# Chunk 0's second layer by Strassen's identity, and a later load of five sequences' beacon keys

## The chip, the cores and the metric

The kernel runs on one core of one Trainium2 chip. The metric is the device time of one execution in microseconds (us). A core has five engines with a queue of instructions each: PE (TensorE, matmuls; its weight loads are listed apart as PEld), DVE (VectorE), ACT (ScalarE), POOL (GpSimd) and SP (SyncE, which only issues transfers here). Engines wait for each other by semaphores; within a queue the order of the program is kept.

## The reference

Attention over 8 sequences of 8 heads, 576 positions and width 64, with 16 beacon keys and values per head that every position may see, and then two dense layers over all 4608 positions:

```python
k_all = np.concatenate([beacon_k, k], axis=2)
v_all = np.concatenate([beacon_v, v], axis=2)
scores = scale * np.matmul(q, k_all.transpose(0, 1, 3, 2))
causal[:, Nb:] = np.triu(np.ones((S, S), dtype=bool), k=1)
scores = np.where(causal, -1000000000.0, scores)
a = softmax(scores)                                      # over the keys
x = np.matmul(a, v_all).transpose(0, 2, 1, 3).reshape(B * S, H * D)   # 4608 x 512
h = x @ w_in                                             # 512 x 2048
g = np.maximum(0.01 * h, h)
return (g @ w_out).astype(np.float32)                    # 4608 x 512
```

## The kernel before

**Attention.** Heads go in 32 pairs, four to a sequence: pairs 0 to 3 are sequence 0, pairs 12 to 15 sequence 3. A pair's queries and keys are turned so that the width lies on the partitions: for pairs 0 to 7 by PE (`t_q`), from pair 8 on by SP's transposing transfers (`turn_pair`, L179) out of `q_nat` and `k_nat`, which POOL's casting transfers load (`load_natural`, L171). The 16 beacon keys take the first 16 columns of a pair's key tile. They come from `bkT`, which holds all sequences' beacon keys turned: `load_beacon_k` (L185) loads them, `cast_beacon_k` (L188) makes them bf16, `beacon_transposes` turns them, two PE transposes a sequence (L194) and two DVE copies out of PSUM (L203), and `beacon_columns` (L229, on POOL) copies a pair's 16 columns. Sequences 0 and 1 are loaded at the start, 2 to 7 in one load behind the first half of `w_out`.

From pair 8 on, scores are made in tiles of 512 columns that run on from one pair into the next; a `block` is three tiles (PE L314, exp on ACT L329 and L333), followed by the causal masks on POOL (`triangle`, L289). `value` multiplies with the values (PE L359), and DVE normalises (L388, L389). The result is turned into `xT` by PE for pairs up to 7 (L405, copy L410), by SP's transfers after that (L417, L425).

**Dense layers.** The 4608 positions go in nine chunks of 512. The first layer (`moe1`, L442) makes one block of 128 of the 2048 inner columns in a step, four 128x512 matmuls, and ACT's Prelu writes it to `gT` (L450). The second layer of chunks 1 to 8 follows Strassen's identity in Winograd's form on 2 x 2 blocks: seven products instead of eight. `PRODUCTS` is their order; a product is two steps (one for each 128 tokens) of eight 128x256 matmuls (L544). Its operands are blocks of `gT` and `w_out_sb` or sums of them: `weight_sums` makes t1, t2, t4 (`w_sum`) and overwrites b12 in `w_out_sb` with b22 - b12; `token_sums` makes s1, s2, s4 (`gsum`) and overwrites a21 in `gT` with a11 - a21, in two slices, one for each half of the first-layer blocks. `combine` puts the products together (ACT copies L575, DVE additions L572) and stores four quarters of the chunk. Chunk 0's second layer is plain: `moe2_plain` makes 128 tokens in four steps of four 128x512 matmuls (L519), DVE copies the bank (L528), and SP stores it (L529). `weight_sums(0)` stands at `t0`, behind pair 7's turning, and `weight_sums(1)` behind chunk 0's last step.

**Order.** The order on all engines is written out by hand up to pair 7 (strings that `run` reads: `u` is a first-layer step, `d` a second-layer step, `s` scores, `m` masks, `v` values, `x` turning a pair's result, `T` turning a pair's inputs, `b` beacon columns, `N` loads, `t` weight sums). From pair 8 on it is a list of events sorted by a due place, measured in pairs; between two events first- and second-layer steps (`up`, `down`) are filled in so that the steps that are open are spread evenly. `up` and `down` each issue one waiting DVE sum (`add_due`) ahead of their matmuls. `late` holds additions that are put off to the next step. PSUM has four single banks (`ps_one`) for everything but the scores' double banks.

Of the kernel before, what the change touches and what calls it, by code (L numbers as in the profile page):

```python
# [15 lines left out]
def kernel(  # L16
# [11 lines left out]
    nc = tc.nc  # L28
# [433 lines left out]
    def weight_sums(part):  # L462
        b11, b12 = w_out_sb[:, 0:HF, 0:HD], w_out_sb[:, 0:HF, HD:DM]
        b21, b22 = w_out_sb[:, HF:NF, 0:HD], w_out_sb[:, HF:NF, HD:DM]
        t1, t2, t4 = (w_sum[:, i] for i in range(3))
        tt = nc.vector.tensor_tensor
        if part == 0:
            tt(out=t1, in0=b12, in1=b11, op=SUB)
            tt(out=t2, in0=b22, in1=t1, op=SUB)
            tt(out=t4, in0=b21, in1=t2, op=SUB)  # L470
        else:
            tt(out=b12, in0=b22, in1=b12, op=SUB)
# [3 lines left out]
    def token_sums(i, lo, hi):  # L476
        if i not in sums:
            sums[i] = [sum_tile(n).rearrange("p (c t) -> p c t", c=HF) for n in range(3)]
        g, s = gT[i], sums[i]
        a11, a12 = g[:, lo:hi, 0:HT], g[:, HF + lo : HF + hi, 0:HT]  # L480
        a21, a22 = g[:, lo:hi, HT : 2 * HT], g[:, HF + lo : HF + hi, HT : 2 * HT]
        s1, s2, s4 = (s[n][:, lo:hi] for n in range(3))
        return [
            dict(out=s1, in0=a21, in1=a22, op=ADD),
            dict(out=s2, in0=s1, in1=a11, op=SUB),
            dict(out=a21, in0=a11, in1=a21, op=SUB),
            dict(out=s4, in0=a12, in1=s2, op=SUB),
        ]

# [18 lines left out]
    PRODUCTS = (1, 4, 6, 2, 7, 5, 3)  # L508
    banks, parts = {}, {}

    def ND(i):
        return NF if i == 0 else 2 * len(PRODUCTS)

    def moe2_plain(i, t, quarter):
        if quarter == 0:
            banks["a"] = ps_one.tile([128, 512], FP32, name="acc", tag="one")
        acc = banks["a"]
        for fc in range(quarter * 4, quarter * 4 + 4):
            nc.tensor.matmul(  # L519
                out=acc,  # L520
                lhsT=gT[i][:, fc, t * 128 : (t + 1) * 128],
                rhs=w_out_sb[:, fc],
                start=(fc == 0),
                stop=(fc == NF - 1),
            )
        if quarter == 3:
            osb = opool.tile([128, DM], FP32, name=("p1", "p4", "p5", "u3")[t], bufs=1)
            nc.vector.tensor_copy(out=osb, in_=acc)  # L528
            nc.sync.dma_start(out=out[i * 512 + t * 128 : i * 512 + (t + 1) * 128], in_=osb)  # L529

    def moe2(i, n2):
        if i == 0:
            moe2_plain(i, n2 // 4, n2 % 4)
            if n2 == NF - 1:
                weight_sums(1)
            return
        n, tile = PRODUCTS[n2 // 2], n2 % 2
# [16 lines left out]
        elif tile == 1:  # L554
            combine(i, n, acc, (0, 2))
# [3 lines left out]
    def add_late(now=False):  # L559
        while late and (now or late[0][0] < done1[0] + done2[0]):  # L560
            late.pop(0)[1]()

# [231 lines left out]
    def up():  # L794
# [11 lines left out]
        if i1 and n % (2 * SLICE) == 2 * SLICE - 1:  # L806
# [107 lines left out]
    with order:  # L914
# [18 lines left out]
        load_beacon_k(2, B, nc.gpsimd)  # L933
        run("s5.0 s5.1 m5.0 u u u s5.2 s5.3 q6 k6 m5.1 m5.2 o1 u u s6.0 s6.1 m6.0 u v4.0 u v4.1 y4 N8.0 N8.1 u s6.2 s6.3 q7 k7 m6.1 m6.2 u")
        cast_beacon_k(2, B, nc.gpsimd.tensor_copy)
        run("u v5.0 u v5.1 N9.0 s7.0 s7.1 m7.0 d x5 v6.0 v6.1 T8 d s7.2 s7.3")
        beacon_transposes(2, B)
        run("m7.1 m7.2 N9.1 u b8.2 b9.2 b10.2 b11.2 x6 v7.0 T9 v7.1 d d d N10.0 N10.1 d V2.0 V2.1 x7 t0 T10")
# [27 lines left out]
        for g in range(FIRST, NG):  # L966
# [5 lines left out]
            if g > FIRST + 3:  # L972
                events.append((g - 2.5, 0, run, ("b%d.2" % g,)))
# [15 lines left out]
        for b in range(2, B):  # L989
            for n in range(2 if b == 2 else 0, NKB):  # L990
                events.append((4 * b + ((-0.1, 0.1)[n > 3] if b == 2 else 0.3 * n - 0.4), 6, load_v_cast, (b, n)))
        events.sort(key=lambda e: e[:2])
# [49 lines left out]
```

## Time and profile before

| what | value |
|---|---|
| median of 3 executions | 325.34 us (325.18 to 329.55) |
| the profiled execution | 325.64 us, of which the span of the instructions is 323.8 us |
| granted TensorE clock | 1.0 |
| chunk 0's second layer | 47.3 to 73.5 us |
| scores of block 3 (with pair 11's first columns) | 77.1 to 78.5 us |
| POOL, 58 to 64 and 76 to 88 us | busy the whole time |
| DVE, 53.7 to 78.5 us | busy 11.3 of 24.8 us |
| first product of chunk 1 | from 88.4 us |

The span is cut into 40 slices, with each engine's busy share in tenths:

```
PE   7999999999999999999999999999999999999995
DVE  3464245508255244444443454525464689577954
ACT  4968962387855786478746874687458547455510
POOL 8895868999996787659875977666221000000000
```

In the lists of groups and in the timelines a row has the start, the length, the engine, the line, the operation with its tiles and shapes, the count, and in brackets the idle time ahead of it with what ended it. Matmuls are pipelined: a row's length holds the tail of its last matmul, so lengths are read from one start to the next. In the chain of work that ended last, a row has start, length and what the time was spent on.

### The profile page before, as it was taken

The page shows a single profiled execution, that of the slowest core. Times are in us where ns is not written, and L with a number is a line of the kernel's source. Part 1 is how long each engine was busy: PE and PEld are TensorE (multiplying, and loading weights), DVE is VectorE, ACT ScalarE, POOL GpSimd, SP SyncE. Part 2 cuts the span into 40 slices and gives each one's busy share as a digit, 9 for nine tenths or more (in the row PEclk, how much of TensorE's full clock was granted, in tenths as well). Part 3 has the DMA queues.
Part 4 walks back from the last instruction along what each step waited for, and adds up shares of the span by engine and source line. Part 5 has one row for each costly group of instructions (what it writes and reads, how often), then busy time and mean ns, then how long its engine had stood idle before and what let it go on. Part 6 is the DMA issues. An engine that isn't in the chain of part 4 may idle for free.

```text
span 323.8 us, 8701 instructions
## 1 busy us (share of the span) xinstructions
PE 314.3 (97%) x3468; PEld 219.1 (68%) x3494; DVE 168.0 (52%) x341; ACT 203.8 (63%) x346; POOL 184.3 (57%) x354
## 2 busy tenths in 40 slices
PE   7999999999999999999999999999999999999995
PEld 4575555444588557855788888656875697688784
DVE  3464245508255244444443454525464689577954
ACT  4968962387855786478746874687458547455510
POOL 8895868999996787659875977666221000000000
PEclk9999999999999999999999999999999999999999
DMA  8999999999999999999999999999222100200123
GB/s 137 129 189 192 124 214 140 169 177 188 135 152 160 216 138 129 114 186 97 141 176 174 99 143 119 188 128 129 44 81 82 26 2 32 75 25 2 65 67 130
DMA packets 155256, 39.78 MB, mean 123 GB/s; under 512 B 142368, under 2 KB 152480, under 8 KB 155216
## 3 DMA queue, kind: packets, MB, share of 16 engines
q0 software_dynamic: 99824, 18.54, 91.1%
q1 hardware_dynamic: 55120, 20.62, 38.3%
q8 instruction: 27, 0.44, 0.6%
q14 instruction: 13, 0.11, 0.1%
q10 hardware_dynamic: 272, 0.07, 0.1%
HBM read 37.22 MB, written 9.44 MB: 144 GB/s over the span
## 4 chain that ended last, share of the span: by engine, by line
PE 72%; DMA 14%; POOL 9%; ACT 3%; issue 1%; DVE 0%; POOLq 0%; ACTq 0%; SPq 0%
PE acc L442 24%; PE acc L544 19%; PE sc L544 11%; PE av L359 6%; PE sc L314 5%; PE acc L663 5%; DMA w_out_sb<-in_moe_w_out_dram 4%; DMA gsum<-in_k_dram 4%; POOL aT L289 3%; DMA k_nat<-in_k_dram 3%; DMA v_aug<-in_v_dram 2%; ACT aT L333 2%; DMA kT<-k_nat 2%; POOL gsum L158 1%; POOL v_aug L214 1%
## 5 line engine op out<-in xcount | busy, mean ns | idle before, releaser
L442 PE MATMUL acc<-xT,w_in_sb 128*128 128x512 bf16 (+1 forms) x537 | 116.5, 354 | 1.5 <-ACT aT L329 0.3
L450 ACT ACTIVATE gT<-acc 128x512 bf16<-128x512 f32 x124 | 70.8, 623 | 33.1 <-PE acc L442 32.6
L289 POOL TENSOR_SCALAR_AFFINE_SELECT aT<-aT 128x256 bf16<-128x256 bf16 (+2 forms) x160 | 59.7, 403 | 51.4 <-ACT aT L329 31.5
L442 PEld LDWEIGHTS <-w_in_sb 128*128 128x128 bf16 x560 | 51.7, 98 | 43.9 <-issue 2.9
L544 PEld LDWEIGHTS <-gT 128*128 128x128 bf16 x512 | 48.7, 98 | 7.7 <-issue 1.8
L333 ACT ACTIVATE aT<-sc 128x1024 bf16<-128x1024 f32 (+3 forms) x64 | 51.7, 892 | 0.0
L329 ACT ACTIVATE aT<-sc 128x512 bf16<-128x512 f32 (+3 forms) x64 | 29.0, 520 | 27.8 <-PE sc L314 27.8
L388 DVE RECIPROCAL rec<-av 128x6 f32<-128x6 f32 (+1 forms) x64 | 12.0, 187 | 65.0 <-PE av L359 64.4
L359 PEld LDWEIGHTS <-aT 128*128 128x128 bf16 (+1 forms) x960 | 36.9, 98 | 9.2 <-issue 1.4
L544 PEld LDWEIGHTS <-gsum 128*128 128x128 bf16 x384 | 36.5, 98 | 6.5 <-issue 0.4
L359 PE MATMUL av<-v_aug,aT 128*128 128x65 bf16 (+1 forms) x960 | 39.8, 194 | 0.8 <-DMA v_aug<-in_v_dram 0.4
L214 POOL DMA_DIRECT2D v_aug<-in_v_dram x40 | 34.1, 856 | 4.2 <-DMA w_in_sb<-in_moe_w_in_dram 3.8
L171 POOL DMA_DIRECT2D k_nat<-in_k_dram x48 | 34.8, 730 | 0.9 <-DMA w_out_sb<-in_moe_w_out_dram 0.3
L171 POOL DMA_DIRECT2D q_nat<-in_q_dram x48 | 34.8, 729 | 0.6 <-issue 0.4
L389 DVE TENSOR_TENSOR x_nat<-av,rec 128x384 bf16<-128x384 f32 (+1 forms) x64 | 31.4, 491 | 2.2
L544 PE MATMUL acc<-w_out_sb,gT 128*128 128x256 bf16 x240 | 28.9, 273 | 0.4 <-ACT gT L450 0.4
L276 ACT ACTIVATE aT<-sc 128x1024 bf16<-128x1024 f32 (+3 forms) x32 | 26.0, 874 | 4.7 <-PE sc L267 2.5
L314 PE MATMUL sc<-qT,kT 64*128 64x80 bf16 (+22 forms) x384 | 22.2, 250 | 0.3
L314 PEld LDWEIGHTS <-kT 64*128 64x128 bf16 x384 | 12.8, 94 | 11.2 <-issue 7.6
L544 PE MATMUL acc<-w_sum,gsum 128*128 128x256 bf16 x160 | 20.1, 273 | 0.0
L575 ACT COPY p<-acc 128x512 f32<-128x512 f32 x15 | 9.1, 604 | 16.8 <-PE acc L544 16.8
L785 DVE TENSOR_TENSOR gsum<-gT 128x1024 bf16<-128x1024 bf16 x16 | 11.0, 688 | 15.7 <-ACT gT L450 15.7
(95 smaller groups left out, 339.0 us busy)
## 6 DMA issues: line engine op xcount, KB each, us to landing
out_dram<-p SPq DMA_DIRECT2D x26, 256.0 KB, 3.2
q_nat<-in_q_dram POOLq DMA_DIRECT2D x48, 72.0 KB, 5.5
k_nat<-in_k_dram POOLq DMA_DIRECT2D x48, 72.0 KB, 5.3
v_aug<-in_v_dram POOLq DMA_DIRECT2D x24, 128.0 KB, 6.5
w_in_sb<-in_moe_w_in_dram POOLq DMA_DIRECT2D x2, 1024.0 KB, 12.4
w_out_sb<-in_moe_w_out_dram POOLq DMA_DIRECT2D x2, 1024.0 KB, 12.1
out_dram<-u SPq DMA_DIRECT2D x8, 256.0 KB, 2.7
gsum<-in_q_dram POOLq DMA_DIRECT2D x8, 144.0 KB, 7.1
```

The lines of the kernel that those rows point to most:

```text
L171: nc.gpsimd.dma_start(out=t[:, :, par], in_=(q, k)[which][b, 2 * hp + par].rearrange("(t p) d -> p t d", p=NR),)
L214: nc.gpsimd.dma_start(out=dst[lo : ROWS[c], c, :, 0:D], in_=v[b, :, OFF[c] : OFF[c] + n].rearrange("h p d -> p h d"),)
L276: nc.scalar.activation(out=aT[:, :, c0 : c0 + w], in_=sc[:, :, 0:w], func=AF.Exp, scale=0.125)
L289: nc.gpsimd.affine_select(out=view, in_=view, compare_op=ALU.is_ge, fill=0.0, base=128 - n if lo == 0 else 0, channel_multiplier=-1, patte ...
L314: nc.tensor.matmul(out=(sc[par] if apart else sc[:, par])[:, at : at + b - a], lhsT=kT[ps_, c * 128 : (c + 1) * 128], rhs=qT[ps_, q0 : q0 ...
L329: nc.scalar.activation(out=probs[g][:, par, lo:hi], in_=sc[par][:, at : at + hi - lo], func=AF.Exp, scale=0.125)
L333: nc.scalar.activation(out=probs[g][:, :, lo:hi], in_=sc[:, :, at : at + hi - lo], func=AF.Exp, scale=0.125)
L359: nc.tensor.matmul(out=avv[:, n, 0 : D + 1], lhsT=aT[0 : ROWS[c], par, a0 : a0 + 128], rhs=va[0 : ROWS[c], c, 2 * hp + par, :], start=(c = ...
L389: nc.vector.tensor_tensor(out=x_nat[:, t0:t1].rearrange("p t e d -> p (t e) d"), in0=avv[:, :, 0:D], in1=rec[:, n0:n1, None].to_broadcast( ...
L442: nc.tensor.matmul(out=acc[:, lo:hi], lhsT=w_in_cols(fc, j), rhs=xT[:, j, x0 : x0 + hi - lo], start=(j == 0), stop=(j == NJ - 1), skip_gro ...
L450: nc.scalar.activation(out=gT[i][:, fc, :], in_=acc, func=AF.Prelu, alpha=0.01)
L544: nc.tensor.matmul(out=acc[:, lo : lo + HD], lhsT=left(i, n, fc, tile), rhs=right(n, fc), start=(lo == 0 and fc == 0), stop=(fc == HF - 1) ...
```

## The change

Chunk 0's second layer takes the seven products too, in an order of its own (`FIRST_PRODUCTS`) and with a combination of its own (`combine_first`). Its token sums are made as soon as half of the first-layer blocks are there and again after the rest, with s4 ahead of a11 - a21. The four weight sums are spread over chunk 0's steps: t1 ahead of pair 8's turning, t2 behind pair 7's turning, b22 - b12 behind product 6's addition, t4 behind product 7's. Chunk 0 has 14 second-layer steps instead of 16, and as the steps are spread by their number, nine instead of eight of chunk 1's first-layer steps stand ahead of block 3's scores. The load of sequence 2's beacon keys stays; that of sequences 3 to 7 is issued between pair 13's query and key loads, cast behind block 3's masks and turned between the two halves of pair 9's values. The beacon columns of pairs 12 to 15 move behind that.

```diff
--- before.py
+++ after.py
@@ -466,10 +466,12 @@
         tt = nc.vector.tensor_tensor
         if part == 0:
             tt(out=t1, in0=b12, in1=b11, op=SUB)
+        elif part == 1:
             tt(out=t2, in0=b22, in1=t1, op=SUB)
+        elif part == 2:
+            tt(out=b12, in0=b22, in1=b12, op=SUB)
+        else:
             tt(out=t4, in0=b21, in1=t2, op=SUB)
-        else:
-            tt(out=b12, in0=b22, in1=b12, op=SUB)
 
     sums = {}
 
@@ -480,12 +482,13 @@
         a11, a12 = g[:, lo:hi, 0:HT], g[:, HF + lo : HF + hi, 0:HT]
         a21, a22 = g[:, lo:hi, HT : 2 * HT], g[:, HF + lo : HF + hi, HT : 2 * HT]
         s1, s2, s4 = (s[n][:, lo:hi] for n in range(3))
-        return [
+        ops = [
             dict(out=s1, in0=a21, in1=a22, op=ADD),
             dict(out=s2, in0=s1, in1=a11, op=SUB),
             dict(out=a21, in0=a11, in1=a21, op=SUB),
             dict(out=s4, in0=a12, in1=s2, op=SUB),
         ]
+        return ops if i else [ops[n] for n in (0, 1, 3, 2)]
 
     def left(i, n, fc, tile):
         t = slice(tile * 128, (tile + 1) * 128)
@@ -505,36 +508,14 @@
         fc0, d0 = {1: (0, 0), 2: (HF, 0), 3: (HF, HD), 7: (0, HD)}[n]
         return w_out_sb[:, fc0 + fc, d0 : d0 + HD]
 
-    PRODUCTS = (1, 4, 6, 2, 7, 5, 3)
+    FIRST_PRODUCTS, PRODUCTS = (1, 2, 3, 5, 6, 7, 4), (1, 4, 6, 2, 7, 5, 3)
     banks, parts = {}, {}
 
     def ND(i):
-        return NF if i == 0 else 2 * len(PRODUCTS)
-
-    def moe2_plain(i, t, quarter):
-        if quarter == 0:
-            banks["a"] = ps_one.tile([128, 512], FP32, name="acc", tag="one")
-        acc = banks["a"]
-        for fc in range(quarter * 4, quarter * 4 + 4):
-            nc.tensor.matmul(
-                out=acc,
-                lhsT=gT[i][:, fc, t * 128 : (t + 1) * 128],
-                rhs=w_out_sb[:, fc],
-                start=(fc == 0),
-                stop=(fc == NF - 1),
-            )
-        if quarter == 3:
-            osb = opool.tile([128, DM], FP32, name=("p1", "p4", "p5", "u3")[t], bufs=1)
-            nc.vector.tensor_copy(out=osb, in_=acc)
-            nc.sync.dma_start(out=out[i * 512 + t * 128 : i * 512 + (t + 1) * 128], in_=osb)
+        return 2 * len(PRODUCTS)
 
     def moe2(i, n2):
-        if i == 0:
-            moe2_plain(i, n2 // 4, n2 % 4)
-            if n2 == NF - 1:
-                weight_sums(1)
-            return
-        n, tile = PRODUCTS[n2 // 2], n2 % 2
+        n, tile = (PRODUCTS if i else FIRST_PRODUCTS)[n2 // 2], n2 % 2
         apart = i == NCH - 1 and n2 >= 10
         if tile == 0 or apart:
             banks["p"] = one_bank()
@@ -552,13 +533,48 @@
         if apart:
             combine(i, n, acc[:, 0:HD], (tile, tile + 1))
         elif tile == 1:
-            combine(i, n, acc, (0, 2))
+            (combine if i else combine_first)(i, n, acc, (0, 2))
 
     late = []
 
     def add_late(now=False):
         while late and (now or late[0][0] < done1[0] + done2[0]):
             late.pop(0)[1]()
+
+    def combine_first(i, n, acc, tiles):
+        def part(name, new=False):
+            if new:
+                parts[name] = opool.tile([128, 512], FP32, name=name, bufs=1)
+            return parts[name]
+
+        def add(to, x, y):
+            nc.vector.tensor_tensor(out=to, in0=x, in1=y, op=ADD)
+
+        if n in (1, 3, 5):
+            nc.scalar.copy(out=part({1: "p1", 3: "p5", 5: "p4"}[n], True), in_=acc)
+        elif n == 2:
+            add(part("u3", True), acc, part("p1"))
+            store(i, 0, 0, tiles, part("u3"))
+        elif n == 6:
+            add(part("u2", True), acc, part("p1"))
+            weight_sums(2)
+        elif n == 7:
+            add(part("p1"), acc, part("u2"))
+            weight_sums(3)
+            p1, p4, p5, u2 = (part(name) for name in ("p1", "p4", "p5", "u2"))
+
+            def rest():
+                add(p5, p5, p4)
+                add(p5, p5, u2)
+                store(i, 0, 1, tiles, p5)
+                add(part("u3", True), p1, p4)
+                store(i, 1, 1, tiles, part("u3"))
+
+            late.append((done1[0] + done2[0], rest))
+        elif n == 4:
+            add_late(True)
+            add(part("p4"), acc, part("p1"))
+            store(i, 1, 0, tiles, part("p4"))
 
     def combine(i, n, acc, tiles):
         lo, hi = tiles[0] * HD, tiles[1] * HD
@@ -803,7 +819,9 @@
         add_due()
         done1[0] += 1
         turn[0] = 1
-        if i1 and n % (2 * SLICE) == 2 * SLICE - 1:
+        if i1 == 0 and n >= HF and n % SLICE == SLICE - 1:
+            due.extend((i1, op) for op in token_sums(i1, n + 1 - SLICE - HF, n + 1 - HF))
+        elif i1 and n % (2 * SLICE) == 2 * SLICE - 1:
             due.extend((i1, op) for op in token_sums(i1, n // 2 + 1 - SLICE, n // 2 + 1))
 
     def down():
@@ -930,12 +948,12 @@
         run("q0.1 k0 w2.384 s0.0 m0.0 w3.256 s0.1 q1 s0.2 m0.1 k1 s0.3 m0.2")
         run("w2.384 s1.0 m1.0 q2 s1.1 k2 w2.384 s1.2 m1.1 w2.384 s1.3 m1.2 W0.0.4 s2.0 m2.0 W0.0.4 s2.1 W0.0.6 q3 l5.0 l5.1 s2.2 k3 w4.384 v0.0 m2.1 s2.3 i1 m2.2 W0.1.4 s3.0 m3.0 v1.0 s3.1 v0.1 s3.2 v1.1 m3.1 l6.0 l6.1 s3.3 x0.1 m3.2")
         run("v2.0 V1.0 V1.1 q4 v2.1 x1 k4.1 v3.0 v3.1 x2.1 s4.0 s4.1 x3 m4.0 V1.2 V1.3 V1.4 l7.0 l7.1 u u s4.2 s4.3 q5 k5 m4.1 m4.2 u o0 u")
-        load_beacon_k(2, B, nc.gpsimd)
+        load_beacon_k(2, 3, nc.gpsimd)
         run("s5.0 s5.1 m5.0 u u u s5.2 s5.3 q6 k6 m5.1 m5.2 o1 u u s6.0 s6.1 m6.0 u v4.0 u v4.1 y4 N8.0 N8.1 u s6.2 s6.3 q7 k7 m6.1 m6.2 u")
-        cast_beacon_k(2, B, nc.gpsimd.tensor_copy)
-        run("u v5.0 u v5.1 N9.0 s7.0 s7.1 m7.0 d x5 v6.0 v6.1 T8 d s7.2 s7.3")
-        beacon_transposes(2, B)
-        run("m7.1 m7.2 N9.1 u b8.2 b9.2 b10.2 b11.2 x6 v7.0 T9 v7.1 d d d N10.0 N10.1 d V2.0 V2.1 x7 t0 T10")
+        cast_beacon_k(2, 3, nc.gpsimd.tensor_copy)
+        run("u v5.0 u v5.1 N9.0 s7.0 s7.1 m7.0 d x5 v6.0 v6.1 t0 T8 d s7.2 s7.3")
+        beacon_transposes(2, 3)
+        run("m7.1 m7.2 N9.1 u b8.2 b9.2 b10.2 b11.2 x6 v7.0 T9 v7.1 d d d N10.0 N10.1 d V2.0 V2.1 x7 t1 T10")
 
 
         FIRST = 2 * NPAIR
@@ -970,7 +988,7 @@
             if g > FIRST + 2:
                 events.append((g - 1.75, 0, run, ("T%d" % g,)))
             if g > FIRST + 3:
-                events.append((g - 2.5, 0, run, ("b%d.2" % g,)))
+                events.append((g - (2.5 if g >= FIRST + 2 * NPAIR else 0.38), 0, run, ("b%d.2" % g,)))
             at = g + (2.05 if g % NPAIR == NPAIR - 1 else 2.25)
             events.append((at, 3, value, (g, 0)))
             events.append((at + 0.37, 4, value, (g, 1)))
@@ -989,6 +1007,9 @@
         for b in range(2, B):
             for n in range(2 if b == 2 else 0, NKB):
                 events.append((4 * b + ((-0.1, 0.1)[n > 3] if b == 2 else 0.3 * n - 0.4), 6, load_v_cast, (b, n)))
+        events.append((FIRST + 1.85, 0, load_beacon_k, (3, B, nc.gpsimd)))
+        events.append((FIRST + 3.45, 0, cast_beacon_k, (3, B, nc.gpsimd.tensor_copy)))
+        events.append((FIRST + 3.6, 0, beacon_transposes, (3, B)))
         events.sort(key=lambda e: e[:2])
         first_down[0] = 4
         w, d0 = 0, done1[0] + done2[0]
```

## The prediction

> **What bounds the kernel now.** I read the engines' shares first, then the chain that ended last, then PE's, DVE's and POOL's timelines between 44 and 90 us, where the change lies. The page gives the bound:
>
> ```profile
> PE 314.3 (97%) x3468; PEld 219.1 (68%) x3494; DVE 168.0 (52%) x341; ACT 203.8 (63%) x346; POOL 184.3 (57%) x354
> PE 72%; DMA 14%; POOL 9%; ACT 3%; issue 1%; DVE 0%; POOLq 0%; ACTq 0%; SPq 0%
> ```
>
> PE is the bound, so what counts is PE's time and any new hole in it. The chain, in order of time, says where PE takes over:
>
> ```profile
> 39.96 13.69 DMA w_out_sb<-in_moe_w_out_dram
> ...
> 64.21 8.28 DMA k_nat<-in_k_dram
> 72.49 0.02 SPq L179
> 72.51 0.03 issue
> 72.54 5.26 DMA kT<-k_nat
> 77.80 0.05 issue
> 77.85 0.67 PE sc L314 x10
> ...
> 88.60 1.75 PE acc L544 x16
> ```
>
> Up to 77.85 us POOL's queue and its loads set the pace (pair 11's keys land at 77.80), afterwards nearly PE alone. Chunk 0's second layer runs from 47.3 to 73.5 us, ahead of that point. In PE's timeline it is the L519 rows:
>
> ```profile
> 53.70 3.61 PE L519 MATMUL acc<-w_out_sb,gT 128*128 128x512 bf16 x15
> 57.15 0.42 PE L405 MATMUL tp<-ident,x_nat 112*128 112x112 bf16 x5
> ...
> 62.27 1.02 PE L442 MATMUL acc<-xT,w_in_sb 128*128 128x512 bf16 x3 [0.27 <-ACT aT L329]
> 63.13 1.03 PE L519 MATMUL acc<-w_out_sb,gT 128*128 128x512 bf16 x4
> 63.99 1.03 PE L442 MATMUL acc<-xT,w_in_sb 128*128 128x512 bf16 x4
> ...
> 77.12 1.39 PE L314 MATMUL sc<-qT,kT 64*128 64x96 bf16 x16
> ```
>
> Starts count here: four L519 matmuls fill 63.13 to 63.99, 0.867 us a step. The scores at 77.12 take 1.39 us where the other three blocks take 0.8: 0.54 us is the wait for pair 11's keys.
>
> **The multiplication saved.** 16 plain steps x 0.867 = 13.87 us go. 14 Strassen steps of eight 128x256 matmuls come; sixteen such take 1.75 us at 88.60, 0.875 a step, 12.25 us. PE gains **1.62 us**. Weight loads go from 64 to 112 of 98 ns (L544's weight-load row); at 109 ns a matmul they stay hidden, as they do at 88.60.
>
> The Trainium skill, "TensorE: Matmul & The Clock Gate", section "Back-to-back issue gap", speaks against this: sustained, it gives about 131 ns for 512 columns and 81 for 128, so narrower matmuls cost more per column. By it, 64 x 131 = 8.4 us would become 112 matmuls of an estimated 98 ns, 11.0 us, a loss of 2.6. The rows say 217 and 109 ns, and I go by them.
>
> **The new waits.** The plain layer needed nothing of DVE but four copies. Now each product needs sums that DVE makes in order, and in chunk 0 the products follow each other without the work that stands between them later. DVE's durations are there:
>
> ```profile
> 55.62 0.69 DVE L528 COPY p<-acc 128x512 f32<-128x512 f32 x1 [1.32 <-PE acc L519]
> ...
> 60.49 1.23 DVE L470 TENSOR_TENSOR w_sum<-w_out_sb,w_sum 128x2048 bf16<-128x2048 bf16 x1
> ...
> 74.31 2.30 DVE L472 TENSOR_TENSOR w_out_sb<-w_out_sb 128x2048 bf16<-128x2048 bf16 x1
> ...
> 77.85 0.69 DVE L785 TENSOR_TENSOR gsum<-gT 128x1024 bf16<-128x1024 bf16 x1
> ```
>
> A token sum is 0.69, an add out of PSUM 0.69 (L572), a weight sum 1.23 us. The copy at 55.62 starts 0.19 us after its eight matmuls (53.70 + 8 x 0.217) are through; I use that 0.19 for PE to DVE and 0.05 back.
>
> The clock starts alike. Steps 1 and 2 still wait for the first half of w_out at 47.30. Before the third, PE has ten transposes less (12 fill 50.73 to 51.18, so 0.37 us), but ACT's new copy of product 1 (0.60) now stands ahead of pair 7's last exps, which started at 50.77; pair 7's last masks and so its values come some 0.4 later. Product 2 starts at 53.75 instead of step 3 at 53.70. Then:
> - **Product 3** reads s4. Behind pair 7's normalising DVE does s1, s2 (to 55.9), the add of product 2 (to 56.6), s4 (to 57.2). PE ends product 2 at 55.50; the first four matmuls use the earlier half of s4 and cover 0.44. Hole: 1.3 us.
> - **Product 6** reads t2, which stands behind the copy of pair 7's transposes, and these follow product 3: 58.83 + 0.19 + 0.46 + 1.23 = 60.7. Product 5 covers 58.83 to 60.58. Hole: 0.1.
> - **Product 7** reads b22 - b12, made behind product 6's add: 62.43 + 0.19 + 0.69 + 1.23 = 64.5. Block 0's scores (0.85), a first-layer step (0.87) and its 0.27 wait cover up to 64.4. Hole: 0.15. If the sum takes the 2.30 of its row, 1.25.
> - **Product 4** reads t4, behind product 7's add: 68.07 + 0.19 + 0.69 + 1.23 + 0.05 = 70.25. Only one first-layer step (0.87) covers it. Hole: 1.3.
>
> Together 2.85, and three times 0.1 for the weight load (98 ns) that isn't hidden when PE starts again: **3.15 us**. Queued behind the waiting matmuls is all of PE; the scores of blocks 0 to 3 then come 1 to 2 us later, ACT's exps and POOL's masks with them.
>
> Why 2.30 for the same shape that took 1.23? At that time POOL runs this, where five masks otherwise take 1.73 (87.12):
>
> ```profile
> 74.78 2.79 POOL L289 TENSOR_SCALAR_AFFINE_SELECT aT<-aT 128x256 bf16<-128x256 bf16 x5
> ```
>
> Both are 1.06 us too long: they stood in each other's way. In the changed order the sum falls at 63.3 to 64.5, where POOL issues loads until 65.67, beside which t4 took its 1.23. I take 1.23. The skill's "SBUF — State Buffer", "Who interferes with whom", says that a DVE operation with two SBUF inputs and a GpSimd one that reads SBUF exclude each other, the first one keeping the port to its end. By that the sum, which began first, would have kept 1.23; it did not, so the first to start isn't safe.
>
> **Beacon keys.** One DMA more on POOL, for five sequences, inside its full stretch from 53.7 to 98 us: at most the 0.85 us of the six-sequence issue. The cast (0.50 for six) shrinks early and returns late, and four column copies of 0.19 move back. POOL loses about 1.2 us near 74 to 84, but waits at block 3's masks anyway, which follow PE. PE does the ten transposes (0.45) between pair 9's two halves. They wait for the cast, which stands behind block 3's masks: scores start + 0.4, exps 3.2, masks 0.6, cast 0.5 = 4.7 us; PE has its scores, four first-layer steps and pair 9's first values in front, also 4.7. I take 0.2. From below it is 0; from above, if the load needs the 10.7 us of today's bk_raw (issued about 73.8, landed 84.5), 0.8. The early gain (640 fewer rows of 64 floats ahead of the second half of w_out, which POOL waits for 0.34 us at 53.94) I cost at nothing: masks set PE's start there. SP gets three stores of 0.53 ahead of pair 12's transposes; they fit behind pair 11's keys at 72.54 + 1.2.
>
> **Sum.** Up to the end of block 3's scores the changed kernel has 12 steps of 0.875 and 9 first-layer steps, before it was 14 of 0.867 and 8: -1.64 + 0.87 = -0.77. Add 3.15 in holes, take off the 0.54 for pair 11's keys and 0.16 at 71.99, add the 0.05: +1.73, so 78.51 becomes 80.2. After it PE has one first-layer step less (-0.87) and the ten transposes with their wait (+0.65): **+1.5 us**. The profiled execution took 325.64 (span 323.8 and 1.8 around it), 0.30 over the median of 325.34. 325.64 + 1.5 = 327.1, or 326.8 on the median's footing: **326.8**.
>
> **Rivals.**
> - *DVE is in time* (0.20). DVE is busy 11.3 of the 24.8 us from 53.7 to 78.5, so there is room; against it, its order has each add in front of the sum that is needed. Then pair 11's keys set the time: PE reaches them earlier, they still land near 77.8, and only the -0.87 + 0.65 behind them and up to 1 us of an earlier POOL remain: 325.1 down to 324.1. This is faster than before; it decides if the holes add up to less than about 1.6 us.
> - *DVE and POOL collide* (0.25). If the masks meet b22 - b12 and t4, each sum takes 1.07 more, as at 74.31, and the masks too: 326.8 + 2.1 = 328.9. It decides if POOL is through with its loads about 1.5 us earlier than today's 65.67.
> - *The cast stops POOL* (0.05). If the beacon load lands late, POOL's queue stands with masks, value loads and pair 15's loads behind it. With the 13.7 us of the second half of w_out it lands at 87.5: +3.6, 330.4; over 2% only if the feed of the next pairs is lost as well.
> - The forecast itself, 325.6 to 328: 0.50.
>
> The range goes from 324.3 to 329.8. Two per cent, about what a measurement of this kernel can tell from no change, is 6.5 us; no case reaches that on the fast side, and only the third could on the slow one: faster 0.01, same 0.94, slower 0.05.
>
> **What would show it.** In the profile after: matmuls of the 128x256 form at 109 ns; PE rows of chunk 0 that wait for DVE, over 1 us at the first s4 and at t4, little at b22 - b12 (a 1.2 us row there, not 2.3); scores of block 3 ending near 80 us with no wait for keys. If these ended before 78.5, the holes are wrong; if the holes are there and the time still falls, the stretch up to 78 us didn't set the end. A wait of PE or POOL for bk_raw over 0.8 us would speak for the third rival.

## The result, and the profile after

The changed kernel takes 328.19 us in the median of 22 executions (326.48 to 333.54), the kernel before, run between them, 325.27 us (22 executions, 323.57 to 330.25). Five of the first and two of the second were slow (over 1.5% above the kernel's fastest; in one of them, whose profile came with the result, PE ran at little more than half its pace for the first 24 us, thirteen matmuls in 1.57 us instead of 0.90), and the ratio leaves such executions out: **1.0079, 95% interval 1.0061 to 1.0098**. It was measured twice more, beside the experiments: 1.0070 (1.0045 to 1.0095) and 1.0069 (1.0046 to 1.0092). So the change costs some 2.2 to 2.6 us; the forecast was 1.5, 326.8 with a range of 324.3 to 329.8.

The rows here are from another execution of the changed kernel, "o_after": 327.09 us, span 325.1. The engines, from its page:

```profile
PE 313.3 (96%) x3517; PEld 223.4 (69%) x3542; DVE 174.0 (54%) x354; ACT 205.3 (63%) x349; POOL 187.4 (58%) x356
```

PE is busy 1.0 us less than before (314.3) while the span is 1.3 us longer (325.1 against 323.8): PE waits more. Where it waits is in its timeline (start, length, engine, line, operation, count, and in brackets the idle time ahead of the row with what ended it):

```profile
51.67 1.91 PE L525 MATMUL acc<-w_out_sb,gT 128*128 128x256 bf16 x16
53.42 0.60 PE L525 MATMUL acc<-w_out_sb,gsum 128*128 128x256 bf16 x4
55.10 1.48 PE L525 MATMUL acc<-w_out_sb,gsum 128*128 128x256 bf16 x12 [1.08 <-DVE gsum L801]
...
62.36 1.05 PE L525 MATMUL acc<-w_out_sb,gT 128*128 128x256 bf16 x8 [0.17 <-DVE w_out_sb L472]
...
68.19 1.03 PE L525 MATMUL acc<-w_sum,gT 128*128 128x256 bf16 x8 [1.14 <-DVE w_sum L474]
...
71.50 0.72 PE L314 MATMUL sc<-qT,kT 64*128 64x256 bf16 x10 [0.32 <-DMA kT<-k_nat]
...
77.51 0.83 PE L314 MATMUL sc<-qT,kT 64*128 64x96 bf16 x16
...
92.81 0.56 PE L314 MATMUL sc<-qT,kT 64*128 64x384 bf16 x6 [1.58 <-POOL kT L229]
```

Sixteen matmuls fill 51.67 to 53.42, 109 ns each. The holes are 1.08 us for s4, 0.17 for b22 - b12, 1.14 for t4. Then come two waits that the forecast hadn't: 0.32 us for pair 10's keys and **1.58 us for the beacon column of pair 13**. The two other profiles of the changed kernel have the same holes to 0.01 us and the same 1.58, but no wait for pair 10's keys. On POOL the column, a copy of 0.22 us, has this ahead of it:

```profile
88.01 2.80 POOL L289 TENSOR_SCALAR_AFFINE_SELECT aT<-aT 128x256 bf16<-128x256 bf16 x5
90.76 1.78 POOL L214 DMA_DIRECT2D v_aug<-in_v_dram  x2
92.53 0.22 POOL L229 COPY kT<-bkT 128x16 bf16<-128x16 bf16 x1
```

Block 4's masks and two value loads, 4.5 us, stand in the queue before a copy that PE needs for the very next scores. In the kernel before, POOL made this copy at 77.53 us and PE began these scores at 90.28:

```profile
77.53 0.19 POOL L229 COPY kT<-bkT 128x16 bf16<-128x16 bf16 x1
...
90.28 0.85 PE L314 MATMUL sc<-qT,kT 64*128 64x16 bf16 x16
```

**A cut at the end of block 3's scores.** The forecast split its sum there, and the split proves sharp. Before, block 3's scores end at 78.51 us and 245.25 us of the span remain. After, they end at 78.34 (77.51 + 0.83) and 246.77 remain. In three profiles of kernels whose program is the same from there on (before, and two experiments below) the remainder is 245.25, 245.24 and 245.24 us (spans of 323.76, 324.86 and 322.37 us, to two places from the traces); in the other two profiles of the changed kernel it is 246.8 and 247.5, and in the second of these only the last store is later. So its +1.5 is no noise. What lies ahead of the cut moves by a microsecond or more from one execution to the next: chunk 0's second layer began at 47.30 us in the profile before, at 45.59 here.

### The profile page after: what moved, and what is told of

Same layout as the page of the kernel before. It is cut to its first block, busy times and chain, and to the rows that moved or that the text cites. A ratio compares the mean times of both kernels' runs of the same rounds, so it can differ in the third digit from the quotient of the medians.

```text
span 331.8 us, 8820 instructions
## 1 busy us (share of the span) xinstructions
PE 320.4 (97%) x3517; PEld 226.3 (68%) x3542; DVE 174.4 (53%) x354; ACT 206.1 (62%) x349; POOL 188.9 (57%) x356
## 4 chain that ended last, share of the span: by engine, by line
PE 91%; DVE 2%; ACT 2%; POOL 2%; issue 1%; ACTq 0%; POOLq 0%
PE acc L442 30%; PE acc L525 21%; PE sc L525 11%; PE av L359 9%; PE sc L314 6%; PE acc L679 5%; PE sc L267 3%; PE av L843 3%; PE tp L243 2%; ACT aT L333 1%; POOL aT L289 1%; PE tp L405 1%; PE av L855 1%; DVE gsum L801 1%; POOL v_aug L214 0%
## 5 line engine op out<-in xcount | busy, mean ns | idle before, releaser
L289 POOL TENSOR_SCALAR_AFFINE_SELECT aT<-aT 128x256 bf16<-128x256 bf16 (+2 forms) x160 | 62.6, 419 | 60.4 <-ACT aT L329 30.0
L450 ACT ACTIVATE gT<-acc 128x512 bf16<-128x512 f32 x124 | 70.8, 625 | 33.3 <-PE acc L442 32.9
L525 PEld LDWEIGHTS <-gT 128*128 128x128 bf16 x576 | 54.6, 98 | 11.8 <-issue 4.0
L333 ACT ACTIVATE aT<-sc 128x1024 bf16<-128x1024 f32 (+3 forms) x64 | 51.7, 890 | 0.9 <-PE sc L314 0.9
L525 PEld LDWEIGHTS <-gsum 128*128 128x128 bf16 x432 | 40.9, 98 | 8.5 <-DVE gsum L801 1.4
L525 PE MATMUL acc<-w_out_sb,gT 128*128 128x256 bf16 x288 | 35.1, 273 | 0.8 <-ACT gT L450 0.7
L276 ACT ACTIVATE aT<-sc 128x1024 bf16<-128x1024 f32 (+3 forms) x32 | 26.8, 875 | 7.3 <-PE sc L267 7.0
L525 PE MATMUL acc<-w_sum,gsum 128*128 128x256 bf16 x192 | 23.9, 273 | 0.0
L801 DVE TENSOR_TENSOR gsum<-gT 128x1024 bf16<-128x1024 bf16 x18 | 12.4, 691 | 16.4 <-ACT gT L450 16.4
```

Of the source, the lines that this page charges most:

```text
L276: nc.scalar.activation(out=aT[:, :, c0 : c0 + w], in_=sc[:, :, 0:w], func=AF.Exp, scale=0.125)
L289: nc.gpsimd.affine_select(out=view, in_=view, compare_op=ALU.is_ge, fill=0.0, base=128 - n if lo == 0 else 0, channel_multiplier=-1, patte ...
L333: nc.scalar.activation(out=probs[g][:, :, lo:hi], in_=sc[:, :, at : at + hi - lo], func=AF.Exp, scale=0.125)
L450: nc.scalar.activation(out=gT[i][:, fc, :], in_=acc, func=AF.Prelu, alpha=0.01)
L525: nc.tensor.matmul(out=acc[:, lo : lo + HD], lhsT=left(i, n, fc, tile), rhs=right(n, fc), start=(lo == 0 and fc == 0), stop=(fc == HF - 1) ...
```

## The experiments

The theory at the start was that of the forecast: PE's time and PE's holes set the pace, Strassen's holes cost more than it saves. Rival A: in the stretch up to block 3 the transfers that turn the keys (SP, L179) run at nearly PE's pace, so PE time saved or lost there is mostly not passed on. The table has all kernels; "pair 10's keys" is from the issue of the turning transfer to its landing, in that kernel's one profile; the medians are of all executions, the ratios as above; "rest" is the span behind the end of block 3's scores.

| kernel | median us | ratio to before (95%) | pair 10's keys, us | block 3's scores end | rest |
|---|---|---|---|---|---|
| before | 325.2 to 325.3 | | 62.3 to 70.1 | 78.51 | 245.2 |
| a_strassen | 326.71 | 1.0039 (1.0012–1.0066) | 62.5 to 71.4 | 79.45 | 245.2 |
| b_beacon | 327.49 | 1.0053 (1.0024–1.0081) | 64.1 to 71.6 | 80.07 | 246.7 |
| c_sums | 328.53 | 1.0096 (1.0062–1.0130) | 62.3 to 71.3 | 78.32 | 246.7 |
| d_columns | 327.05 | 1.0063 (1.0035–1.0092) | 62.2 to 70.8 | 78.82 | 246.3 |
| f_sums_early | 327.70 | 1.0078 (1.0057–1.0098) | 62.4 to 73.1 | 80.04 | 244.8 |
| i_offload | 327.14 | 1.0063 (1.0038–1.0087) | 61.4 to 70.1 | 77.09 | 248.3 |
| j_shift | 327.38 | 1.0067 (1.0041–1.0093) | 63.8 to 71.2 | moved | moved |
| n_less | 324.87 | 1.0003 (0.9980–1.0027) | 61.0 to 71.6 | 79.62 | 245.2 |
| l_late | 326.77 | 1.0043 (1.0003–1.0082) | 62.7 to 69.6 | 80.31 | 244.6 |
| m_before_late | 325.32 | 1.0011 (0.9981–1.0041) | 61.0 to 67.8 | 77.14 | 245.2 |
| o_after | 327.30 | 1.0069 (1.0046–1.0092) | 61.1 to 71.4 | 78.34 | 246.8 |

### Each half alone

*a_strassen* is the changed kernel with the beacon keys as before; *b_beacon* is the kernel before with only the beacon part. Against the changed kernel, a_strassen is:

```diff
-        load_beacon_k(2, 3, nc.gpsimd)
+        load_beacon_k(2, B, nc.gpsimd)
-        cast_beacon_k(2, 3, nc.gpsimd.tensor_copy)
+        cast_beacon_k(2, B, nc.gpsimd.tensor_copy)
-        beacon_transposes(2, 3)
+        beacon_transposes(2, B)
-                events.append((g - (2.5 if g >= FIRST + 2 * NPAIR else 0.38), 0, run, ("b%d.2" % g,)))
+                events.append((g - 2.5, 0, run, ("b%d.2" % g,)))
-        events.append((FIRST + 1.85, 0, load_beacon_k, (3, B, nc.gpsimd)))
-        events.append((FIRST + 3.45, 0, cast_beacon_k, (3, B, nc.gpsimd.tensor_copy)))
-        events.append((FIRST + 3.6, 0, beacon_transposes, (3, B)))
```

and b_beacon is the reverse of these lines, in the kernel before.

> The changed kernel with the beacon keys as before (one load for sequences 2 to 7, turned early, columns at their old places), so the Strassen part alone. Theory 1 (the time is lost in PE's waits for DVE's sums, about 1.1 us at s4 and 1.1 at t4, and the beacon part costs nothing): as slow as the changed kernel, 327.6 us (+0.7%). Theory 2 (the beacon part costs what the changed kernel is slower by: 1.6 us in the wait for pair 13's beacon column and some 0.6 for the ten later transposes): 325.5, within 0.2% of the kernel before. Both together, as the profile after reads: the holes of 1.1 stay, the 1.6 goes, 326.0 (+0.2%).

> The kernel before with the later beacon load alone; chunk 0's second layer plain. Theory 1: the beacon part costs nothing, 325.3 us. Theory 2: +1.5 to +2.2 us, 327.0, with a wait of scores for a beacon column on POOL of over 1 us. In between, if the later load frees the DMA engines ahead of 53 us: down to 324.8.

Strassen alone costs 0.4%, 1.3 us; the later beacon load alone 0.5%, 1.7 us. Together that is a little over what both cost at once. The table's last column gives them different places: Strassen leaves the rest at 245.2 although one first-layer step (0.87) went from it, the beacon part puts it at 246.7. In b_beacon that is 0.45 us of transposes, 0.22 of waiting for the cast and 0.56 for pair 13's column, not the 1 us and more that its theory 2 expected; 0.3 us is left over. In a_strassen's timeline of PE the first two rows here bound the stretch that Strassen changes, and the third has the wait that eats most of its gain in the rest:

```profile
53.39 1.92 PE L525 MATMUL acc<-w_out_sb,gT 128*128 128x256 bf16 x16
...
78.61 0.83 PE L314 MATMUL sc<-qT,kT 64*128 64x96 bf16 x16
...
85.78 0.61 PE L314 MATMUL sc<-qT,kT 64*128 64x512 bf16 x6 [0.58 <-DMA kT<-k_nat]
```

From the start of product 2 to the end of block 3's scores PE takes 26.06 us here; in the kernel before, from the same place (the third step, 53.70), it took 24.81, with the 0.54 for pair 11's keys in it. The holes are there (0.95, 0.17 and 1.14), and PE waits for no keys in this stretch. d_columns below and the two other profiles of the changed kernel repeat it: 26.18 us each, again without a wait for keys. So in these four PE with its holes sets the end, as the forecast had it, and Strassen costs 1.25 to 1.37 us there.

The wait of 0.58 us is for pair 12's keys. Their transfer went out at 78.4 us and landed at 85.7; before, it went out at 76.6 and landed at 80.6. Chunk 0's results now leave as three stores in a row on SP, ahead of pair 12's turning; o_after's SP timeline shows the same:

```profile
73.57 0.53 SPq L618 DMA_DIRECT2D out_dram<-p  x1
74.20 0.42 SPq L618 DMA_DIRECT2D out_dram<-u  x1
74.71 0.50 SPq L618 DMA_DIRECT2D out_dram<-p  x1
75.37 2.13 SPq L179 DMA_TRANSPOSE qT<-q_nat  x1
```

Before, the turning of pair 12's queries started at 74.9 and took SP 1.2 us; here it starts at 75.37 and takes 2.13, so that of the keys starts late. The stores delay it by their place; whether they also make it longer was not tried apart (turnings of 2.1 to 2.6 us stand in other places too, without such a row of stores: n_less has one of 2.38 at 52.30).

### The holes closed

*c_sums* takes the holes for s4 and t4 away: product 5, which reads t2, comes before product 3, and t4 is made directly behind b22 - b12.

```diff
-    FIRST_PRODUCTS, PRODUCTS = (1, 2, 3, 5, 6, 7, 4), (1, 4, 6, 2, 7, 5, 3)
+    FIRST_PRODUCTS, PRODUCTS = (1, 2, 5, 3, 6, 7, 4), (1, 4, 6, 2, 7, 5, 3)
...
             weight_sums(2)
+            weight_sums(3)
         elif n == 7:
             add(part("p1"), acc, part("u2"))
-            weight_sums(3)
```

> The changed kernel with product 5 ahead of product 3, so that s4 has a product's time more, and t4 made right behind b22 - b12 and so ahead of product 7's addition. Theory 1: the PE waits for s4 and t4 (1.08 and 1.14 us in the profile after) are gone, the time falls by 2.0 to 2.4 us to 325.6. Theory 2, that PE then waits elsewhere (pair 11's keys, or the beacon column, which POOL sets and not PE): the time falls by less than 1 us, 327.0, and the wait for pair 13's column grows to 2.5 us or more.

It got no faster: 1.0096. The holes are gone from PE's timeline, and other waits stand there instead (c_sums):

```profile
71.47 0.72 PE L314 MATMUL sc<-qT,kT 64*128 64x256 bf16 x10 [1.03 <-POOL aT L289]
...
83.01 0.47 PE L194 MATMUL tp<-ident,bk 128*64 128x128 bf16 x10 [0.77 <-POOL bk L188]
...
92.75 0.56 PE L314 MATMUL sc<-qT,kT 64*128 64x384 bf16 x6 [0.76 <-POOL kT L229]
```

The first names POOL's masks, but pair 10's turned keys landed at 71.3 us, and those are what these scores read: they start 0.13 us after it, as they do after the landing in f_sums_early and o_after. Pair 8's keys (landed at 60.87) cost another 0.47 us, at 60.96. Block 3's scores end at 78.32, against 78.34 with the holes. This was the first sign that PE's holes are not all there is. But product 2 also began later here, at 52.96 us against 51.67 in o_after; counted from it, the closed holes gave 1.3 us, or 0.8 against the 26.18 above, of their 2.4.

*f_sums_early* is c_sums with the beacon keys as before (the lines of a_strassen).

> Both sums moved (product 5 ahead of product 3, t4 behind b22 - b12) and the beacon keys as in the kernel before. Theory A (up to 78 us the turned keys set the pace, not PE; afterwards PE alone): PE waits about 1 us at block 2's scores for pair 10's keys, which land near 71; block 3's scores start at 77.1 to 77.6, as before; behind them there is one first-layer step less (-0.87): 324.5 to 325.0 us. Theory B (PE alone sets the time, and the holes were the whole loss): the full saving of 1.6 us and no wait at block 2: 323.7. Theory C (the three stores of chunk 0 in a row ahead of pair 12's turning make its keys land near 85.7 instead of 80.6): a new wait of 0.5 to 1.5 us at block 4's scores, 325.3 to 326.

Again no gain: 1.0078, and the wait for pair 10's keys is larger. The chain that ended last, of f_sums_early, shows the keys' transfer right ahead of the scores (start, length, what):

```profile
62.37 10.69 DMA kT<-k_nat
73.06 0.14 issue
73.19 0.72 PE sc L314 x10
```

PE stood still for 2.54 us ahead of that row. From the end of block 2's scores to the end of block 3's it then takes 6.11 to 6.13 us in a, c, d, f, i, l and o: wherever PE waited for pair 10's keys at block 2 (c, f, i, o), block 3 simply follows their landing; in a, d and l it follows PE.

### The columns, and the beacon work elsewhere

*d_columns* is the changed kernel with the columns of pairs 13 to 15 right behind pair 12's, ahead of block 4's masks on POOL.

```diff
-                events.append((g - (2.5 if g >= FIRST + 2 * NPAIR else 0.38), 0, run, ("b%d.2" % g,)))
+                events.append((g - 2.5 if g >= FIRST + 2 * NPAIR else FIRST + 3.62 + 0.001 * (g % NPAIR), 0, run, ("b%d.2" % g,)))
```

> The changed kernel with the beacon columns of pairs 13 to 15 copied right behind pair 12's, ahead of the value loads and the masks. Theory 2: the wait of 1.58 us for pair 13's column is gone, 326.2 us (-1.6). Theory 1: PE has no slack before it anyway and the wait moves to another thing that POOL issues late; 327.8, as the changed kernel.

The wait of 1.58 us is gone, but the rest falls by only 0.5 us, from 246.8 to 246.3, for there are three others (d_columns, PE):

```profile
85.63 0.61 PE L314 MATMUL sc<-qT,kT 64*128 64x512 bf16 x6 [0.57 <-DMA kT<-k_nat]
...
92.25 0.56 PE L314 MATMUL sc<-qT,kT 64*128 64x384 bf16 x6 [0.23 <-DMA kT<-k_nat]
...
102.86 0.35 PE L359 MATMUL av<-v_aug,aT 80*128 80x65 bf16 x6 [0.42 <-DMA v_aug<-in_v_dram]
```

They add up to 1.22 us. They were not hidden behind the column's wait: pair 12's and 13's keys landed at 84.39 and 88.31 us in o_after, in time for their scores, and at 85.49 and 92.11 us here, though pair 12's turning was issued at the same time (77.67 and 77.51). Whether the moved columns make them later can't be told from one profile each. The ratio, 1.0063, can't be told from the changed kernel's.

*i_offload* is c_sums with the late beacon work off POOL: the load on SP, the cast and the columns on DVE.

```diff
-                events.append((g - (2.5 if g >= FIRST + 2 * NPAIR else 0.38), 0, run, ("b%d.2" % g,)))
+                events.append((g - 2.5, 0, run, ("b%d.2" % g,)) if g >= FIRST + 2 * NPAIR else (FIRST + 3.62 + 0.001 * (g % NPAIR), 0, run, ("b%d.0" % g,)))
...
-        events.append((FIRST + 1.85, 0, load_beacon_k, (3, B, nc.gpsimd)))
-        events.append((FIRST + 3.45, 0, cast_beacon_k, (3, B, nc.gpsimd.tensor_copy)))
+        events.append((FIRST + 1.85, 0, load_beacon_k, (3, B, nc.sync)))
+        events.append((FIRST + 3.35, 0, cast_beacon_k, (3, B, nc.vector.tensor_copy)))
```

> Both sums moved, the later beacon load kept, but issued by SP, cast by DVE and the columns of pairs 12 to 15 copied by DVE, so POOL has none of it. If POOL's queue is what makes the later beacon keys cost: no wait for the cast (0.77 with the sums moved alone) and none for pair 13's column (0.76); block 4's scores start near 83.5 instead of 84.9, 325.0 us, 1.5 to 2 less than with the sums moved alone. If it's the load's place, not its engine: waits of PE for DVE instead, 326.5.

It has the earliest end of block 3's scores of all Strassen forms (77.09; its product 2 began at 51.98) and the longest rest (248.3): PE waits 1.19 us for DVE's cast at 82.21 and 1.75 us for pair 12's keys at 86.29 (landed 86.2). What was gained ahead of the cut was paid back behind it. The expected 325.0 us did not come: PE's waits moved from POOL's cast and column to DVE's cast and the keys.

*j_shift* is f_sums_early with blocks 2 and 3 a quarter of a pair later, so that dense steps cover pair 10's keys.

```diff
-            events.append((FIRST + (0.4 if m else 0.6) + 1536 / COLS * m, 2, block, (m,)))
+            events.append((FIRST + (0.65 if 1 < m < 4 else 0.4 if m else 0.6) + 1536 / COLS * m, 2, block, (m,)))
```

> As the kernel with both sums moved and the early beacon keys, but blocks 2 and 3 a quarter of a pair later, so that two first-layer steps and pair 8's first values stand ahead of block 2's scores and one step more ahead of block 3's. Theory A: the wait for pair 10's keys is covered by work, as PE is 2.1 us later there, and 0.5 to 1.0 us is gained, 323.8 to 324.3 us. Theory B: no wait was there to cover; the same time as without the shift. If exps and masks come too late for the values: 325.5 or more.

The wait for pair 10's keys is gone, but not the 0.5 to 1.0 us that theory A expected to gain: one of 1.57 us for pair 9's stands at 66.06, and 0.61 for values at 103.44. The ratio, 1.0067, can't be told from f_sums_early's.

*g_after* and *o_after* are the changed kernel without an edit, for further ratios and profiles.

> The changed kernel as it is, for a profile whose first 25 us are not disturbed. If the profile read so far holds: PE waits of about 1.1 us for s4 and for t4, scores of block 3 starting near 78.5 us (77.1 before), a wait of 0.5 to 1.6 us for the beacon column of pair 13 on POOL, 327.8 us. If the column's wait came from the disturbed start alone, it is under 0.2 and the time is 326.3.

> The changed kernel again, for a profile whose first 25 us are not disturbed. Both theories: a span of 326 to 327.5 us, waits of about 1.1 us for s4 and for t4, 0.2 for b22 - b12, 0.5 to 1.6 for pair 13's beacon column, and 328.2 us as the median.

Their ratios stand in the first section, and o_after's rows there too; its median, 327.30, is under the expected 328.2. The column's wait is 1.58 us in all three profiles of the changed kernel, so g_after's first reading holds.

### PE's time taken away

*n_less* asks directly what PE time in this stretch is worth. It is the kernel before with 8 of chunk 0's 64 second-layer matmuls left out (and `stop` set on the last that remains).

```diff
-        for fc in range(quarter * 4, quarter * 4 + 4):
+        for fc in range(quarter * 4, quarter * 4 + (4 if quarter < 3 else 2)):
...
-                stop=(fc == NF - 1),
+                stop=(fc == NF - 3),
```

> The kernel before with 8 of the 64 matmuls of chunk 0's second layer left out (two of the 16 inner blocks for each 128 tokens), which is 8 x 0.217 = 1.73 us less PE work between 47 and 73 us and nothing else; chunk 0's result lacks these blocks. It asks for the value of PE time in this stretch with no Strassen sums and no late beacon in the way. Theory A (the transfers of the turned keys set the pace there along with PE): pair 10's and 11's keys land where they landed, near 70.1 and 77.8 us, PE waits longer for them, and the time falls by 0 to 0.9 us, to 324.4 to 325.3. Theory B (PE's time alone sets the pace, as my sum took it): the time falls by 1.5 to 1.7 us, to 323.6 to 323.8.

324.87 us, a ratio of 1.0003 with an interval from 0.9980 to 1.0027, that is -0.7 to +0.9 us. The 1.73 us that left PE did not arrive. In n_less' timeline of PE there are waits:

```profile
59.45 0.85 PE L314 MATMUL sc<-qT,kT 64*128 64x512 bf16 x12 [1.13 <-DVE w_sum L470]
...
71.72 0.72 PE L314 MATMUL sc<-qT,kT 64*128 64x256 bf16 x10 [2.56 <-DMA kT<-k_nat]
...
78.96 0.67 PE L314 MATMUL sc<-qT,kT 64*128 64x128 bf16 x10 [1.32 <-DMA kT<-k_nat]
```

(The first names a DVE sum; pair 8's turned keys landed at 59.4.) Together 5.0 us for keys, where the kernel before waited 0.54 in the same stretch. This profile is of one of n_less' longer executions (326.80 us, the median is 324.87), so it shows where PE waits, not how long in the median. And the transfers did not follow PE (chain of n_less):

```profile
62.28 10.92 DMA k_nat<-in_k_dram
73.26 5.66 DMA kT<-k_nat
```

Before, pair 11's key load was issued at 64.21 and landed after 8.28 us, at 72.49. Here it was issued 1.9 us earlier and landed 0.7 us later. Rival A holds for the kernel before: in this stretch the arrival of the keys takes back what is taken off PE. Both limits are close, so the longer one sets the end. In us, from the third step or product 2 to the end of block 3's scores:

| kernel | stretch | PE's holes for sums | waits for keys |
|---|---|---|---|
| before | 24.81 | none | 0.54 |
| n_less | 27.78 | none | 5.01 |
| a_strassen | 26.06 | 2.26 | none |
| d_columns | 26.18 | 2.40 | none |
| o_after | 26.67 | 2.39 | 0.32 |
| c_sums | 25.36 | none | 0.47 + 1.03 |
| i_offload | 25.11 | none | 0.27 + 0.99 |
| f_sums_early | 27.28 | none | 0.65 + 2.54 |

With the holes PE is late enough for the keys; without them it meets them.

### The transfers eased

*l_late* is f_sums_early with sequence 2's value loads behind pair 11's key loads on POOL, and product 2's store issued with product 6. *m_before_late* is the kernel before with only the first of these.

```diff
-                events.append((4 * b + ((-0.1, 0.1)[n > 3] if b == 2 else 0.3 * n - 0.4), 6, load_v_cast, (b, n)))
+                events.append((4 * b + (0.45 if b == 2 else 0.3 * n - 0.4), 6, load_v_cast, (b, n)))
...
-            store(i, 0, 0, tiles, part("u3"))
         elif n == 6:
...
             weight_sums(3)
+            store(i, 0, 0, tiles, part("u3"))
```

> f_sums_early (Strassen with early sums, beacon as before) with two transfers moved away from pair 10's keys: product 2's store goes out with product 6 instead of product 2, behind pair 10's turning on SP, and the value loads of sequence 2 that stood ahead of pair 11's key loads on POOL go behind them. Theory A: pair 10's turned keys landed at 73.1 us instead of 70.1 because of the store and the loads next to it; without them the wait of 2.54 us at block 2's scores falls under 0.5 and the time to 325.2 to 326.3. Theory B (the landing follows from the queue and the issue place, not from what stands beside it): keys land within 0.7 us of 73, and the time stays at 327.2 to 328.

> The kernel before with only the later value loads of sequence 2 of l_late. If these loads hold up pair 11's keys, PE's wait of 0.54 us for them goes and the time falls by 0.3 to 0.6 us, to 324.7 to 325.0; if they do not, the time stays within 0.3 us of 325.3. If the values then come late for pair 8's or 9's second halves, it rises.

In both, pair 10's keys took 6.8 to 6.9 us to land, in the other kernels 7.4 to 10.7. In l_late the wait of 2.54 us went as A expected. Yet the time is 326.77, not 325.2 to 326.3, and PE's timeline has two others instead:

```profile
60.99 0.85 PE L314 MATMUL sc<-qT,kT 64*128 64x512 bf16 x12 [1.07 <-issue]
...
66.52 0.78 PE L314 MATMUL sc<-qT,kT 64*128 64x384 bf16 x12 [1.38 <-POOL aT L289]
```

Pair 8's keys landed at 60.9 and pair 9's at 66.4, so these too are waits for keys. A store alone is not the reason for late keys: m_before_late has one at the same place (SP, 58.75) and its pair 10 took 6.8 us. The place of the value loads may be; that rests on one profile each. In m_before_late the 0.54 us wait for pair 11's keys went (0.21 us is left, for DVE), but no gain can be measured: 1.0011 (0.9981 to 1.0041). No version beat the kernel before.

## Why the prediction was right, and where its reasons were not

The time fell into the range and the side was right; the sum was short by about 0.7 to 1.1 us. Its first half, PE with its holes ahead of the cut, came out nearly as worked out; its second half, behind the cut, was wrong by 1.7 us. That the total came so near is in part luck: the first half was too large and the second too small.

- **The multiplication.** The price was right, 109 ns a matmul, and the loss of 2.6 us that the quoted figures for narrow matmuls would have made of it did not show. But a saving of 1.62 us was booked in full. Alone it would hardly have arrived: n_less shows that 1.73 us taken from PE in that stretch shorten the time by at most 0.7, the end of its interval. It counts here only because the holes made PE the longer of the two limits again.
- **The holes.** Right one by one: 1.08 for s4 (forecast 1.3), none listed for t2 (0.1), 0.17 for b22 - b12 (0.15), 1.14 for t4 (1.3). They add up to 2.39, not 2.85. The weight sum b22 - b12 took its 1.22 us, not the 2.30 of its row before:

```profile
60.48 0.69 DVE L551 TENSOR_TENSOR u<-acc,p 128x512 f32<-128x512 f32 x1 [2.02 <-PE acc L525]
61.09 1.22 DVE L472 TENSOR_TENSOR w_out_sb<-w_out_sb 128x2048 bf16<-128x2048 bf16 x1
```

  This is DVE's timeline of o_after: the weight sum stands behind an addition out of PSUM, as the forecast had it; so does t4, at 66.83.
- **Their sum, +1.73 at the end of block 3's scores.** In the four profiles with holes and without a wait for keys it is 1.25 to 1.37, and about 0.5 more in o_after, 0.32 of it a wait for keys; the forecast had 1.68 from product 2 on. So the mechanism held, with holes somewhat smaller than forecast, and block 3's scores ended near 79 us (79.45, 78.82) with no wait for keys, as its signs asked. The medians give 2.2 to 2.6 less the 1.5 behind the cut, some 0.8 to 1.1 us, and a_strassen's 1.3. What does not hold is what would follow if the time were PE's alone, that a closed hole is won. c_sums, f_sums_early, i_offload and j_shift have no hole for a sum, and none is faster than the changed kernel beyond the noise; in their profiles PE waits 1.3 to 3.2 us for keys instead. The forecast's sum had the keys only as the 0.54 us for pair 11's; it did not ask how close to PE's new times those of pairs 8 to 10 land.
- **Behind the cut, -0.87 + 0.65 = -0.2.** This term was mis-sized: measured +1.5 (246.77 against 245.25). The ten transposes take their 0.45 us and the wait of 0.2 for the cast is not in the list of o_after's waits (b_beacon has 0.22). What was missing is 1.58 us for pair 13's column; about 0.4 us more than these terms make (-0.87 + 0.45 + 1.58) is left unexplained. The forecast costed the columns as POOL time, "four column copies of 0.19 move back", and never asked what stands ahead of each copy on POOL when its scores are due.
- **Three stores on SP "fit behind pair 11's keys".** In o_after they just do: pair 12's keys land at 84.39 us, while block 4's scores are under way (84.18 to 85.13). a_strassen and d_columns, where they land at 85.73 and 85.49, wait 0.58 and 0.57 us for them.
- **The rivals.** *DVE is in time* named the right master, the keys, and the wrong pairs and price: with the holes closed the time is 1.0078 and 1.0096, not 324.1 to 325.1, for PE waits for pairs 8, 9 and 10 as soon as it is early. *DVE and POOL collide* didn't happen at the weight sums. *The cast stops POOL* cost nothing in o_after and 0.77 us in c_sums.

What stays open: why a turned key tile lands 6.8 us after its issue in one kernel and 10.7 in another, and why the 0.8 to 1.3 us by which c_sums' profile is shorter in the stretch than those with holes does not show in its median. Its profile is one of its faster executions (326.74 us, the median of all is 328.53), and single profiles differ by as much as that.

## What to carry to other kernels

Where a chain of transfers and the bounding engine end within a microsecond of each other, the later one sets the end: time taken off the engine, or a hole closed, is a gain only down to the transfers. Leave out work of that size once and see what arrives, before a cheaper algorithm is put there. When a small producer is moved late, go through its consumers one by one and read what the queue holds ahead of each; the price is the queue, not the copy. Cut the trace where the bound changes hands: behind the cut the rest repeated to 0.01 us in three profiles here, so that the two halves of a change of under one per cent could be read apart.

## What was not expected of the hardware

- Issuing a transfer earlier did not make it land earlier: pair 11's key load, issued 1.9 us earlier in n_less, landed 0.7 us later. The turning of pair 10's keys, the same transfer each time, took from 6.8 to 10.7 us.
- POOL's masks were slower beside DVE's sums of two SBUF operands, and not beside the weight sum of the kernel before alone: in o_after five masks of one shape take 1.73 us at 75.72 and 2.80 us at 88.01, where token sums (L801) run on DVE from 88.70 on. The token sums themselves kept 0.68 and 0.69 us, but for one of 0.89. The causes are read from the overlap; no run moved the one away from the other.
